# Keys and values of a banded attention, staged beside constants in idle memory and placed by DMA

## The chip, the cores and the metric

The kernel runs on one core of one Trainium2 chip. A core has a matrix engine (TensorE, PE in the profile), a vector engine (VectorE, DVE), an activation engine (ScalarE, ACT), GpSimd (POOL), a sequencer that only issues transfers here (SyncE, SP), 16 DMA engines, an on-chip memory of 128 partitions (SBUF) and eight accumulation banks of 128 x 512 float32 (PSUM) into which TensorE writes. The engines run their own instruction lists in order and wait for each other by semaphores. The metric is the device time of one execution in microseconds, lower is better.

## The reference

Four layers act on one residual stream x of 2048 tokens by 512 features in bfloat16: A, B, A, B, each with a layer norm in front. A is linear attention, B is softmax attention over a band of 256 tokens; both have 32 heads of 16 features.

```python
def _A_ref(x, wqkv, wo):                      # H = 32, Dh = 16
    q, k, v = split_heads(x @ wqkv)
    phi = lambda t: jnp.where(t > 0, t + 1, jnp.exp(t)) + 1e-6
    pq, pk = phi(q), phi(k)
    kv = jnp.einsum("bhsd,bhse->bhde", pk, v); z = jnp.einsum("bhsd->bhd", pk)
    num = jnp.einsum("bhqd,bhde->bhqe", pq, kv)
    den = jnp.einsum("bhqd,bhd->bhq", pq, z)[..., None] + 1e-6
    return merge_heads(num / den) @ wo
def _B_ref(x, wqkv, wo):                      # W = 256
    q, k, v = split_heads(x @ wqkv)
    scores = jnp.einsum("bhqd,bhkd->bhqk", q, k) * (Dh ** -0.5)
    p = _softmax(jnp.where(0 <= iq - ik < W, scores, -1e9))
    return merge_heads(jnp.einsum("bhqk,bhkd->bhqd", p, v)) @ wo
x = x + _A_ref(_layernorm(x), ...); x = x + _B_ref(_layernorm(x), ...)   # twice
```

(`split_heads` and `merge_heads` stand for the reshapes and transposes of the original.)

## The kernel before

**Tiling and stages.** The 2048 tokens are 16 tiles of 128, on the partitions where features are free and the other way round after a transpose. `build` (L325) writes five stages into one graph of operations: `layer_a_keys` (keys, values and queries of the first A layer), `barrier(1)`, `middle(2)`, `barrier(2)`, `middle(3)`. A barrier sums keys times values over all tiles (`a_kv`, L499), masks the sum, multiplies it with the output weights (M, L539) and forms the denominators. A `middle` finishes an A layer tile by tile (`a_out`, then `norm`, then the projections of layer B), runs layer B with the scores of a tile against this tile and the next two, and, in `middle(2)`, the key and value projections of the next A layer (`a_k`, `a_v`).

**Order.** Each operation has a key, in units of tiles (100 times the stage plus the tile plus an offset from PAR, L22), a cost, what it reads and writes, and the PSUM banks it needs. `schedule` (L87) plays the graph forward: each engine takes the ready operation with the smallest key, and operations named by `either` or `copy` go to ACT or DVE, whichever is free first. That gives one fixed order for each engine. `synchronise` (L219) turns it into semaphore waits: one counting semaphore for each compute engine, and one of 48 semaphores for each transfer. SP issues all transfers in order, so a transfer that waits holds those behind it.

**Keys of layer B.** The scores are matrix products with 32 rows in contraction, four side by side in the array. A group of 32 rows holds a pair of heads, so the keys of a pair must stand beside zeros: for each block of 64 tokens `kB` has 128 columns, 64 with only the first head's rows filled and 64 with only the second's. `b_qkv` (L584) projects the keys with the weights `wBp`, which GpSimd has permuted at the start (L403: in a group of 32, 16 rows of one head, then 16 of the other), and one DVE instruction (L595) reads the 128 x 512 result from PSUM twice over, times a per-partition 0 or 1 (`half`, L391 to L394), into the 1024 columns of `kB`. `kB` has four slots, tile t uses slot t % 4.

**Values of layer B.** The product of probabilities and values contracts over 128 rows: 64 tokens for the first head of a pair and the same 64 for the second. So `vB` has, for each block of 64 tokens and each pair, 34 columns: the first head's 16 values and a one in partitions 0 to 63, the second head's 16 values and a one in partitions 64 to 127, zeros elsewhere. GpSimd writes the zeros and ones once (L397 to L399). `b_v` (L597) makes the right layout in PSUM by 16 products with 64 columns each (L608), and two copies of 64 partitions (L614, shown as L444) bring it to `vB`, on ACT or DVE.

**Others that the change touches.** `norm` (L413) runs statistics (L416, L417), adds epsilon on DVE (`eps`, L418), takes the power -1/2 on GpSimd (L419), and normalizes on DVE (L420); a DMA transpose (L426) or TensorE turns the tile. `phi` (L474) is an ACT exponential (L478), a DVE minimum (L479) and a DVE combination (L480). The exponentials of layer B are L644, L645 and L678, its masks L651 and L685. `vA` (16 tiles by 512) holds the values of an A layer: written by `a_v` (L488), read by `a_kv` at the barrier, and idle in between.

Of the kernel before, what the change touches and what calls it, by code (L numbers as in the profile page):

```python
# [6 lines left out]
dt = mybir.dt  # L7
ACT = mybir.ActivationFunctionType
ALU = mybir.AluOpType
# [13 lines left out]
    lat_t=4300, cap_s=8, cap_d=2, cap_e=6, mode=100, sem=35, ring_x=3, wait_s=100, act_bias=-0.064, k_aq2=8.75, k_aq3=-3.0, k_akv=16.63, k_far2=1.412, k_far3=0.95, k_pv2=0.414, k_wo2=-0.276, k_next2=1.1, k_q2=3.26, k_ao2=4.701, k_kv2=2.436, k_v2=0.227, k_av2=17.25, k_ak2=0.108, pe_first2=1, pe_last2=1, k_pv3=0.864, k_wo3=1.497, k_next3=1.814, k_q3=3.411, k_ao3=3.603, k_kv3=2.867, k_v3=0.163, pe_first3=3, pe_last3=1,  # L23
# [23 lines left out]
class Graph:  # L47
    def __init__(self):
        self.ops, self.w, self.r = [], {}, {}
# [37 lines left out]
def schedule(g, par):  # L87
# [39 lines left out]
    while done < len(ops):  # L127
# [18 lines left out]
        for e in engines:  # L146
# [4 lines left out]
            held_back = False  # L151
            while ready[e]:
# [149 lines left out]
class Plan:  # L302
# [22 lines left out]
    def build(self):  # L325
        self.setup()
        self.layer_a_keys(1, 0)
        self.barrier(1)
        self.middle(2)
        self.barrier(2)  # L330
        self.middle(3)
# [6 lines left out]
    def setup(self):  # L338
# [52 lines left out]
        pool("c17", lambda e: e.iota(K.row[:], pattern=[[0, 1]], base=0, channel_multiplier=1), 163, 150, wr=[("row",)])  # L391
        self.on("DVE", "c18", lambda e: e.tensor_scalar(K.row2[:], K.row[:], 4, 1, op0=ALU.logical_shift_right, op1=ALU.bitwise_and), 14, (70, 150), rd=[("row",)], wr=[("row2",)])
        self.on("DVE", "c19", lambda e: e.tensor_copy(K.half[:, 1:2], K.row2[:]), 15, (70, 150), rd=[("row2",)], wr=[("half1",)])
        self.on("DVE", "c20", lambda e: e.tensor_scalar(K.half[:, 0:1], K.half[:, 1:2], -1.0, 1.0, op0=ALU.mult, op1=ALU.add), 16, (70, 150), rd=[("half1",)], wr=[("half",)])  # L394

        for s in range(4):
            pool("c21", lambda e, s=s: e.memset(K.vB[:, s, :, :, :], 0.0), 167, 1100, wr=[("vB", s)])  # L397
            pool("c22", lambda e, s=s: e.memset(K.vB[0:64, s, :, :, 16:17], 1.0), 168, 130, rd=[("vB", s)], wr=[("vB", s)])
            pool("c23", lambda e, s=s: e.memset(K.vB[64:128, s, :, :, 33:34], 1.0), 168, 130, rd=[("vB", s)], wr=[("vB", s)])  # L399
# [13 lines left out]
    def norm(self, t, key, xn_slot, out, wr, by_pe):  # L413
# [4 lines left out]
        self.on("DVE", "eps", lambda e: e.tensor_scalar(K.ve[:, t, :], K.mv[:, t, 1:2], LN_EPS, None, op0=ALU.add), key + 0.02, (66, 150), rd=[("mv", t)], wr=[("ve", t)])  # L418
# [165 lines left out]
    def b_qkv(self, t, s, key, key2):  # L584
# [10 lines left out]
        self.on("DVE", "bke", lambda e: e.tensor_tensor(K.kB[:, r, :, :, :], K.ps(pk).rearrange("p (b n) -> p b n", b=8).unsqueeze(2).to_broadcast([P, 8, 2, 64]), K.half[:].unsqueeze(1).unsqueeze(3).to_broadcast([P, 8, 2, 64]), ALU.mult), key + 0.05, dve(1024), rd=[("half",)], wr=[("kB", r)], ps=[pk])  # L595

    def b_v(self, t, s, key):  # L597
        K = self
        rd = [("xT", s)]
        r = t % 4  # L600
        pv = Tile(1, K.cls)

        def put(e):
            m = None
            for b in range(2):
                for c in range(4):
                    for a in range(2):
                        m = e.matmul(K.ps(pv)[64 * a:64 * a + 64, 256 * b:256 * b + 256], K.xT[:, s, c, 64 * b:64 * b + 64], K.wBv[:, c, 256 * a:256 * a + 256], start=c == 0, stop=c == 3, tile_position=(0, 64 * a))  # L608
            return m

        self.pe("bv", put, key, 8, 256, mode=(128, 64), rd=rd + [("wBv",)], ps=[pv])
        for a in range(2):
            rows = slice(64 * a, 64 * a + 64)
            self.copy("bve", pv, lambda a=a, rows=rows: K.vB[rows, r, :, :, 17 * a:17 * a + 16], lambda rows=rows: K.ps(pv)[rows, :].rearrange("p (b r d) -> p b r d", b=2, d=DH), key + 0.05, 512, wr=[("vB", r, a)], rd=[("vB", r)])  # L614

    def b_scores(self, j, f, key):
# [16 lines left out]
        self.pe("s", put, key, 1, sum(ns), mode=(32, 128), rd=[("kB", j % 4)] + [("XQ", t) for t in range(j, last + 1)], ps=ps)  # L633
# [21 lines left out]
    def b_far(self, j, key):  # L655
# [15 lines left out]
        self.pe("s", put, key, 1, 512, mode=(32, 128), occ=245, rd=[("kB", j % 4), ("XQ", j + 2)], ps=ps)  # L671
# [17 lines left out]
    def b_values(self, j, h, key):  # L689
# [5 lines left out]
        for f in (2 * h, 2 * h + 1):  # L695
# [10 lines left out]
            for i in range(max(0, j - 2), j + 1):  # L706
                rd += [("P", i % 3, f), ("vB", i % 4, 0), ("vB", i % 4, 1), ("vB", i % 4)]
                rd += [("P", i % 3, f, h_, b) for h_ in range(3) for b in (None, 0, 1)]
# [17 lines left out]

    def middle(self, ph):
        K = self
        K.cls = "D"
# [12 lines left out]

        for t in range(min(3, T)):
            front(t)
        self.b_v(0, 0, base - par["k_v"])
        for j in range(T):
# [16 lines left out]
            if last:  # L763
                self.on("SP", "out", lambda e, j=j: e.dma_start(K.out[0, j * P:(j + 1) * P, :], K.xres[:, j, :]), k + 0.1, (600, 2600), rd=[("xres", j)])
            else:
                k += par["k_next"] - par["k_wo"]
                self.norm(j, k, 3, lambda j=j: K.XQ[:, :, j * P:(j + 1) * P], [("XQ", j)], tail)
                self.a_k(j, k + par["k_ak"])
                self.a_v(j, base + par["k_av"] + 0.01 * j)


class Kernel(Plan):
# [16 lines left out]
    def run(self):  # L789
# [4 lines left out]
        with ExitStack() as cx:  # L794
# [7 lines left out]
            sb("stats", [T, 6], F32); sb("mv", [T, 2], F32); sb("ve", [T, 1], F32); sb("rs", [T, 1], F32)  # L802
            sb("ident", [P]); sb("ones", [P]); sb("bmask", [P]); sb("hot", [4, 32]); sb("spread", [4, 4, P]); sb("eps", [32])
            sb("tri", [2, 64]); sb("negh", [1], F32); sb("half", [2], F32); sb("row", [1], dt.int32); sb("row2", [1], dt.int32)
# [88 lines left out]
```

## Time and profile before

| | |
|---|---|
| runs (median of 3; lowest, highest) | 469.32 us; 468.39, 469.47 |
| the profiled execution: its own time; its span | 471.55 us; 469.8 us |
| mean granted TensorE clock | 0.969 |
| busy: PE, DVE, ACT, POOL | 409.5, 405.6, 370.4, 60.4 us |
| weight loads on PE | 284.0 us |
| DMA traffic | 19.11 MB, 41 GB/s in the mean |

Times in rows are microseconds from the start of the span. A group's row has the line, the engine, the operation, what it writes and reads, the shapes, how many (x), then the busy time and the mean of one in ns, then how long the engine stood idle just before such instructions and what released it. A timeline's row has the start, the length, and what ran. Busy times of stretches show which engine is full in which stage; a row of `PE` counts matmuls with their pipeline's end, `PEld` the weight loads.

### The profile page before, as it was taken

What the parts mean: (1) busy time and instruction counts of PE and PEld (TensorE: products, weight loads), DVE (VectorE), ACT (ScalarE), POOL (GpSimd) and SP (SyncE); (2) the same over time, 40 slices, a digit from 0 to 9 for tenths busy, and PEclk for the clock granted to TensorE, in tenths of its full rate; (3) what the DMA queues carried; (4) which work ended last, traced back from release to release, by engine and by line L of the source; (5) the groups of instructions that cost most, each with busy time, mean ns of one, the idle gap of its engine ahead of it and who ended that gap; (6) DMA issues with size and microseconds to landing.
All of it is one profiled execution on the core that took longest, in us unless ns stands there. A gap on an engine that the chain in (4) does not pass through costs nothing.

```text
span 469.8 us, 17818 instructions
## 1 busy us (share of the span) xinstructions
PE 409.5 (87%) x7937; PEld 284.0 (60%) x8004; DVE 405.6 (86%) x923; ACT 370.4 (79%) x550; POOL 60.4 (13%) x114
## 2 busy tenths in 40 slices
PE   3899989988888887999999998879899999998875
PEld 1455668656565555676666765756666657666543
DVE  4998699999999988998998749998999999998653
ACT  2365524989999979889999453599999999999982
POOL 8865000100101010000000000100000000000000
PEclk9899999999999999999999999998999999999776
DMA  8700002011131222122111100021222122121011
GB/s 274 265 0 1 1 1 37 13 32 29 35 37 36 36 36 36 36 37 35 25 26 27 28 9 1 4 22 35 48 25 59 39 35 48 36 47 36 25 33 39
DMA packets 47948, 19.11 MB, mean 41 GB/s; under 512 B 40192, under 2 KB 47360, under 8 KB 47872
## 3 DMA queue, kind: packets, MB, share of 16 engines
q1 hardware_dynamic: 47872, 17.97, 18.5%
q8 instruction: 63, 1.03, 0.9%
q14 instruction: 13, 0.11, 0.1%
HBM read 6.29 MB, written 2.10 MB: 18 GB/s over the span
## 4 chain that ended last, share of the span: by engine, by line
PE 38%; DVE 35%; ACT 20%; issue 2%; POOL 2%; DMA 1%; POOLq 0%
PE ps L455 13%; ACT pb L644 11%; PE ps L469 8%; PE ps L703 7%; DVE stats L416 4%; DVE xres L582 4%; PE ps L608 3%; ACT pb L678 3%; PE ps L630 3%; DVE pb L651 3%; DVE vB L444 3%; DVE kB L595 2%; DVE pqd L576 2%; DVE pb L685 2%; DVE tE L479 2%
## 5 line engine op out<-in xcount | busy, mean ns | idle before, releaser
L644 ACT ACTIVATE pb<-ps 128x1024 bf16<-128x1024 f32 x224 | 212.3, 1038 | 15.8 <-PE ps L630 15.0
L703 PEld LDWEIGHTS ps<-vB,pb 128*128 128x128 bf16 x2880 | 78.7, 96 | 21.7 <-DVE kB L595 3.3
L703 PE MATMUL ps<-vB,pb 128*128 128x34 bf16 x2880 | 84.9, 178 | 6.5 <-DVE o L715 1.4
L419 POOL TENSOR_TENSOR rs<-ve,negh 128x1 f32<-128x1 f32 x64 | 36.6, 571 | 356.2 <-DVE ve L418 354.8
L469 PE MATMUL ps<-xT,wBp 128*128 128x128 bf16 x1024 | 67.6, 220 | 3.5 <-ACT xT L439 1.4
L469 PEld LDWEIGHTS ps<-xT,wBp 128*128 128x128 bf16 x1024 | 58.8, 98 | 15.3 <-DVE xres L582 4.9
L455 PE MATMUL ps<-wA,XQ 128*128 128x512 bf16 x234 | 60.7, 392 | 5.8 <-DVE XQ L439 1.3
L478 ACT ACTIVATE tE<-ps 128x512 bf16<-128x512 f32 x64 | 39.0, 609 | 31.1 <-PE ps L455 14.6
L630 PE MATMUL ps<-XQ,kB 32*128 32x256 bf16 (+3 forms) x1024 | 50.6, 273 | 12.0 <-ACT pb L644 6.5
L651 DVE TENSOR_TENSOR pb<-pb,tri 128x512 bf16<-128x512 bf16 x128 | 53.1, 415 | 8.6 <-ACT pb L645 4.4
L678 ACT ACTIVATE pb<-ps 128x512 bf16<-128x512 f32 x112 | 58.7, 630 | 1.8 <-PE ps L668 1.6
L582 DVE TENSOR_TENSOR xres<-ps,xres 128x512 bf16<-128x512 f32 x64 | 43.7, 682 | 8.0 <-PE ps L455 7.0
L416 DVE BATCH_NORM_STATS2 stats<-xres 128x6 f32<-128x512 bf16 x64 | 43.4, 683 | 3.6 <-DMA xres<-in_A_x_dram 3.0
L595 DVE TENSOR_TENSOR kB<-ps,half 128x1024 bf16<-128x1024 f32 x32 | 38.8, 1211 | 1.3 <-PE ps L469 1.3
L455 PEld LDWEIGHTS ps<-wA,XQ 128*128 128x128 bf16 x256 | 21.9, 100 | 29.3 <-issue 4.1
L685 DVE TENSOR_TENSOR pb<-pb,tri 128x1024 bf16<-128x1024 bf16 x56 | 37.4, 679 | 2.4 <-ACT pb L678 2.4
L630 PEld LDWEIGHTS ps<-XQ,kB 32*128 32x128 bf16 x1024 | 15.3, 93 | 39.0 <-ACT pb L644 19.0
L455 PE MATMUL ps<-wBo,oT 128*128 128x512 bf16 x107 | 32.1, 411 | 7.2 <-DVE pqd L576 1.6
L608 PE MATMUL ps<-wBv,xT 128*64 128x256 bf16 x512 | 35.3, 283 | 1.7 <-DVE o L715 1.3
L479 DVE TENSOR_SCALAR tE<-tE 128x512 bf16<-128x512 bf16 x64 | 20.7, 325 | 17.4 <-ACT tE L478 17.1
L469 PE MATMUL ps<-XQ,wA 128*128 128x128 bf16 x512 | 34.9, 219 | 0.6 <-DVE recf L559 0.6
L444 DVE CAST vB<-ps 64x512 bf16<-64x512 f32 x44 | 30.4, 690 | 3.9 <-PE ps L608 2.5
(81 smaller groups left out, 489.0 us busy)
## 6 DMA issues: line engine op xcount, KB each, us to landing
out_dram<-xres SPq DMA_DIRECT2D x16, 128.0 KB, 1.7
wA<-in_A_wqkv_dram SPq DMA_DIRECT2D x3, 512.0 KB, 5.7
xres<-in_A_x_dram SPq DMA_DIRECT2D x2, 512.0 KB, 8.1
pb<-in_B_wqkv_dram SPq DMA_DIRECT2D x1, 1024.0 KB, 9.9
xres<-in_A_x_dram SPq DMA_DIRECT2D x3, 256.0 KB, 4.4
wAo<-in_A_wo_dram SPq DMA_DIRECT2D x1, 512.0 KB, 8.9
wBv<-in_B_wqkv_dram SPq DMA_DIRECT2D x1, 512.0 KB, 10.0
wBo<-in_B_wo_dram SPq DMA_DIRECT2D x1, 512.0 KB, 9.9
```

Source lines behind the costliest of these rows:

```text
L416: self.on("DVE", "stats", lambda e: e.bn_stats(K.stats[:, t, :], K.xres[:, t, :]), key, dve(512), rd=[("xres", t)], wr=[("stats", t)])
L455: m = e.matmul(K.ps(ps), lhs(c), rhs(c), start=c == 0, stop=c == 3)
L469: m = e.matmul(K.ps(ps)[:, f * P:(f + 1) * P], w(c, f), xT(c), start=c == 0, stop=c == 3)
L582: self.on("DVE", "res", lambda e: e.tensor_tensor(K.xres[:, t, :], K.ps(po), K.xres[:, t, :], ALU.add), key, dve(512), rd=[("xres", t)], w ...
L595: self.on("DVE", "bke", lambda e: e.tensor_tensor(K.kB[:, r, :, :, :], K.ps(pk).rearrange("p (b n) -> p b n", b=8).unsqueeze(2).to_broadca ...
L608: m = e.matmul(K.ps(pv)[64 * a:64 * a + 64, 256 * b:256 * b + 256], K.xT[:, s, c, 64 * b:64 * b + 64], K.wBv[:, c, 256 * a:256 * a + 256], ...
L630: m = e.matmul(K.ps(ps[gq])[:, 256 * b:256 * b + ns[b]], K.kB[rows, j % 4, 2 * f + b, :, :], K.XQ[rows, f, q:q + ns[b]], start=True, stop= ...
L644: return e.activation(x, bank().rearrange("p g (b n) -> p g b n", b=2), ACT.Exp, bias=0.0, scale=0.25)
L651: return e.tensor_tensor(x, x, K.tri[:, 0, :].unsqueeze(1).unsqueeze(1).to_broadcast([P, 4, 2, 64]), ALU.mult)
L678: return e.activation(K.pb[:, sl, 2 * h:2 * h + 2, :, o:o + 64], i, ACT.Exp, bias=0.0, scale=0.25)
L685: return e.tensor_tensor(x, x, K.tri[:, 1, :].unsqueeze(1).to_broadcast([P, 16, 64]), ALU.mult)
L703: m = e.matmul(K.ps(ps)[:, 34 * u:34 * u + 34], K.pb[:, (b // 2) % 3, gq, f, o:o + P], K.vB[:, (b // 2) % 4, b % 2, r, :], start=i == 0, s ...
```

## The change

1. **Keys.** The weights are permuted so that the rows of a pair's two heads alternate (even rows the first head, odd rows the second). One copy (ACT or DVE, `either`) brings the 128 x 512 result into a staging area, in blocks of 64 with 64 constant zeros between them. Two transfers on SP, one for the even partitions and one for the odd, read 1024 columns, the odd ones 64 columns further left, so that zeros fall where the other head's columns are, and write `kB`. 64 rows of 2048 bytes each.
2. **Values.** Plain token-major product (`tok`: four matmuls of 512 columns) in place of 16; one copy of 128 partitions into a second staging area, with 34 columns for each head: 16 values, a constant one, and zeros. Four transfers (block of tokens by head) read 544 columns and write a quarter of `vB`. 64 rows of 1088 bytes each.
3. **Staging area.** It is `vA`, idle in the `middle` stages: tiles 0 to 5 for keys and 6 to 11 for values, two halves each, used in turn. GpSimd writes its zeros and ones at the start of both `middle` stages. `a_v` now stands behind the loop of `middle(2)` in the graph, so that it waits for the last transfer that reads the tiles that it writes.
4. `half`, `row` and the constants of `vB` go away.
5. `eps` goes from DVE to POOL.
6. **Order.** New offsets in PAR for all stages; a second kind of offset (`o_...`) shifts the key of an operation by its name and stage; `wait_s`, which `schedule` uses to hold TensorE back for scores, goes from 100 to 200. (`same` is 0 and does nothing.)

```diff
-    lat_t=4300, ..., wait_s=100, act_bias=-0.064, k_aq2=8.75, k_aq3=-3.0, k_akv=16.63, ...
+    same=0.0, lat_t=4300, ..., wait_s=200, act_bias=-0.378, k_aq2=7.28, k_aq3=-8.85, k_akv=28.47,
+    k_far2=2.522, k_far3=1.248, k_pv2=0.64, ..., k_q2=2.944, k_ao2=4.686, k_kv2=2.41, k_v2=0.148, k_av2=18.49,
+    ..., k_q3=5.029, k_ao3=3.649, k_kv3=2.494, k_v3=-0.211, ..., o_bke3=-0.456, o_ve2=-1.945, o_kd2=-0.187, o_kd3=0.99,
...
-        o = Op(len(self.ops), engs, emit, key, name)
+        o = Op(len(self.ops), engs, emit, key + self.shift.get(name, 0.0), name)
...
-        for s in range(4):
-            pool("c21", lambda e, s=s: e.memset(K.vB[:, s, :, :, :], 0.0), 167, 1100, wr=[("vB", s)])
...
-                    K.wBp[:, q, k, :].rearrange("p (r a d) -> p r a d", a=2, d=DH),
+                    K.wBp[:, q, k, :].rearrange("p (r d a) -> p r a d", a=2, d=DH),
...
-        self.on("DVE", "eps", lambda e: e.tensor_scalar(K.ve[:, t, :], K.mv[:, t, 1:2], LN_EPS, ...), key + 0.02, (66, 150), ...)
+        self.on("POOL", "eps", lambda e: e.tensor_scalar(K.ve[:, t, :], K.mv[:, t, 1:2], LN_EPS, ...), key + 0.02, (190, 260), ...)
...
-        self.on("DVE", "bke", lambda e: e.tensor_tensor(K.kB[:, r, :, :, :], K.ps(pk)...to_broadcast([P, 8, 2, 64]), K.half[:]..., ALU.mult), key + 0.05, dve(1024), ...)
+        flat = lambda: K.vA[:].rearrange("p t d -> p (t d)")[:, 1536 * st:1536 * st + 1152]
+        self.either("bke", lambda e, eng: e.activation(flat()[:, 64:1088].rearrange("p (b a n) -> p b a n", b=8, a=2)[:, :, 0, :], K.ps(pk)..., ACT.Copy) if eng == "ACT" else
+                    e.tensor_copy(flat()[:, 64:1088]...[:, :, 0, :], K.ps(pk)...), key + 0.05, 512, wr=room, ps=[pk])
+        for a in range(2):
+            def put(e, a=a):
+                src, dst = flat(), K.kB[:]
+                ss, ds = src.ap[0][0], dst.ap[0][0]
+                i = bass.AP(src.tensor, src.offset + a * ss + 64 * (1 - a), [[2 * ss, 64], [1, 1024]])
+                o = bass.AP(dst.tensor, dst.offset + a * ds + 1024 * r, [[2 * ds, 64], [1, 1024]])
+                return e.dma_start(o, i)
+            self.on("SP", "kd", put, key + 0.06, (540, K.par["lat_t"]), rd=room, wr=[("kB", r, a)])
...
-        self.pe("bv", put, key, 8, 256, mode=(128, 64), rd=rd + [("wBv",)], ps=[pv])
-        for a in range(2):
-            self.copy("bve", pv, lambda a=a, rows=rows: K.vB[rows, r, :, :, 17 * a:17 * a + 16], ...)
+        pv = self.tok("bv", t, lambda c: K.xT[:, s, c, :], lambda c: K.wBv[:, c, :], [("xT", s), ("wBv",)], key)
+        self.copy("bve", pv, lambda: flat()[:, 17:1105].rearrange("p (h d) -> p h d", d=34)[:, :, 0:16], ..., key + 0.05, 512, wr=room)
+        for b in range(2):
+            for a in range(2):
+                self.on("SP", "vd", lambda e, a=a, b=b: e.dma_start(
+                    K.vB[64 * a:64 * a + 64, r, b, :, :].rearrange("p r d -> p (r d)"),
+                    flat()[64 * b:64 * b + 64, 17 + 527 * a:17 + 527 * a + 544]), key + 0.06, (550, K.par["lat_t"]), rd=room, wr=[("vB", r, a, b)])
...
+        for i in range(2):
+            self.on("POOL", "zero", lambda e, i=i: e.memset(flat(1536 * i, 1152), 0.0), base - 5, (600, 660), wr=self.room[i])
+        for i in range(2):
+            self.on("POOL", "zero", lambda e, i=i: e.memset(flat(3072 + 1536 * i, 1105), 0.0), base - 5, (600, 660), wr=self.roomv[i])
+            self.on("POOL", "zero", lambda e, i=i: e.memset(flat(3072 + 1536 * i + 17, 1088)...[:, :, 16:17], 1.0), base - 5, (150, 200), ...)
...
                 self.a_k(j, k + par["k_ak"])
+        if not last:
+            for j in range(T):
                 self.a_v(j, base + par["k_av"] + 0.01 * j)
```

More of the change, by code (lines that the diff above doesn't have):

```diff
@@ L151, in schedule @@
             held_back = False
+            if e == "PE" and par["same"]:
+                ready[e] = [(ops[i].key + (par["same"] if ops[i].mode != last_mode[0] else 0.0), i) for _, i in ready[e]]
+                heapq.heapify(ready[e])
             while ready[e]:
@@ L611, in b_v @@
-        self.pe("bv", put, key, 8, 256, mode=(128, 64), rd=rd + [("wBv",)], ps=[pv])
-        for a in range(2):
-            rows = slice(64 * a, 64 * a + 64)
-            self.copy("bve", pv, lambda a=a, rows=rows: K.vB[rows, r, :, :, 17 * a:17 * a + 16], lambda rows=rows: K.ps(pv)[rows, :].rearrange("p (b r d) -> p b r d", b=2, d=DH), key + 0.05, 512, wr=[("vB", r, a)], rd=[("vB", r)])
+        st = t % 2
+        room = self.roomv[st]
+        flat = lambda: K.vA[:].rearrange("p t d -> p (t d)")[:, 3072 + 1536 * st:3072 + 1536 * st + 1105]
@@ L631, in put @@
             return m
-        self.pe("s", put, key, 1, sum(ns), mode=(32, 128), rd=[("kB", j % 4)] + [("XQ", t) for t in range(j, last + 1)], ps=ps)
+        self.pe("s", put, key, 1, sum(ns), mode=(32, 128), rd=[("kB", j % 4, 0), ("kB", j % 4, 1)] + [("XQ", t) for t in range(j, last + 1)], ps=ps)
         sl = j % 3
@@ L706, in b_values @@
             for i in range(max(0, j - 2), j + 1):
[L707 removed]
+                rd += [("P", i % 3, f)] + [("vB", i % 4, a, b) for a in range(2) for b in range(2)]
                 rd += [("P", i % 3, f, h_, b) for h_ in range(3) for b in (None, 0, 1)]
@@ L725, in b_out, with phase @@
         self.resid(j, po, key + 0.05)
+    def phase(self, ph):
+        self.g.shift = {k[2:-1]: v for k, v in self.par.items() if k[:2] == "o_" and k[-1] == str(ph)}
     def middle(self, ph):
         K = self
+        self.phase(ph)
         K.cls = "D"
```

49 lines of the change are left out of this document (28 added, 21 removed).

## The prediction

> **What bounds the kernel now.** The page's first table has PE and DVE about equally busy and ACT less, an average over stages with different limits. So I read the busy times of stretches next, cut where the work changes (first column the stretch, second its length; the columns after that as in the first line).
>
> ```profile
> core 0: us, PE busy (x) PEld busy (x) DVE busy (x) ACT busy (x) POOL busy (x), PEclk, DMA share, GB/s
> 0.00:60.00 60.00, 48.08 (x450) 28.23 (x456) 45.88 (x124) 28.97 (x49) 33.04 (x66) 0.97 0.33 106
> 60.00:90.00 30.00, 27.09 (x428) 21.32 (x432) 29.25 (x66) 16.01 (x24) 3.44 (x6) 1.00 0.13 20
> 90.00:250.00 160.00, 140.61 (x3051) 97.87 (x3078) 149.39 (x344) 148.33 (x206) 13.46 (x23) 1.00 0.21 34
> 250.00:282.00 32.00, 31.32 (x495) 22.36 (x500) 19.98 (x50) 19.73 (x46) 1.64 (x3) 1.00 0.07 15
> 282.00:302.00 20.00, 17.11 (x267) 13.04 (x270) 19.85 (x44) 8.36 (x16) 2.19 (x4) 1.00 0.01 2
> 302.00:320.00 18.00, 14.83 (x273) 10.08 (x272) 16.59 (x36) 15.34 (x20) 1.09 (x2) 0.94 0.19 24
> 320.00:430.00 110.00, 102.41 (x2375) 73.45 (x2382) 102.62 (x219) 105.58 (x136) 5.49 (x10) 1.00 0.22 42
> ```
>
> DVE alone is full in 60 to 90 (29.25 of 30) and 282 to 302. In 90 to 250, the steady part of the first middle, DVE and ACT are both at 93%. PE alone is full in 250 to 282, where it makes up the waiting value and query projections. In 320 to 430, the steady part of the second middle, ACT, DVE and PE stand at 96, 93 and 93%.
>
> Which part of ACT can't move is in the groups of its instructions, of 90 to 250 (first row) and 320 to 430 (the others). A tile has four L678 (L673 to L680), so 14 and 11 tiles pass, at 11.4 and 10.0 us each.
>
> ```profile
> L678 ACT ACTIVATE pb<-ps 128x512 bf16<-128x512 f32 x56 | 29.7, 641 | 0.7 <-PE ps L668 0.7
> ...
> L644 ACT ACTIVATE pb<-ps 128x1024 bf16<-128x1024 f32 x87 | 82.1, 1026 | 4.4 <-PE ps L630 4.0
> L678 ACT ACTIVATE pb<-ps 128x512 bf16<-128x512 f32 x44 | 22.7, 618 | 0.1
> ```
>
> The exponentials of the second middle take (82.1 + 22.7) / 11 = 9.53 us of each 10.0: a floor that the change doesn't touch. It can win at most 0.47 us a tile there; the first middle has more room.
>
> **The change part by part.** *What goes and what comes on DVE and ACT.* Rows of the groups, whole run:
>
> ```profile
> L595 DVE TENSOR_TENSOR kB<-ps,half 128x1024 bf16<-128x1024 f32 x32 | 38.8, 1211 | 1.3 <-PE ps L469 1.3
> L444 DVE CAST vB<-ps 64x512 bf16<-64x512 f32 x44 | 30.4, 690 | 3.9 <-PE ps L608 2.5
> L444 ACT ACTIVATE vB<-ps 64x512 bf16<-64x512 f32 x20 | 12.1, 606 | 2.5 <-PE ps L608 1.7
> L444 DVE CAST XQ<-ps 128x512 bf16<-128x512 f32 x18 | 12.3, 683 | 0.4 <-PE ps L469 0.3
> ```
>
> Out of each of the 32 tiles goes one key instruction, 1.21 us, on DVE only, and two value copies, (30.4 + 12.1) / 32 = 1.33 us. In come two copies of 512 columns, of the form of the XQ row: 0.68 on DVE, and on ACT 0.61 as the vB copies there, say 0.65. That saves 1.21 + 1.33 - 1.30 = 1.24 us a tile.
>
> Epsilon leaves DVE. Its row says 144 ns, but the next instruction starts 0.06 us after it:
>
> ```profile
> 66.48 0.14 DVE L418 TENSOR_SCALAR ve<-mv 128x1 f32<-128x1 f32 x1
> 66.54 0.68 DVE L416 BATCH_NORM_STATS2 stats<-xres 128x6 f32<-128x512 bf16 x1
> ```
>
> I count 0.06: two a tile in the first middle, one in the second. A tile is 1.36 and 1.30 us lighter. The POOL epsilon isn't in the trace; POOL's pow on the same shape takes 0.55 (row below), so the chain from statistics to xn grows by at most that, and may shrink by the place in DVE's list that it no longer waits for. It runs over a tile ahead; I take 0.
>
> *TensorE.* Sixteen value matmuls go, four of 512 columns come:
>
> ```profile
> 401.24 1.06 PE L608 MATMUL ps<-wBv,xT 128*64 128x256 bf16 x16
> ...
> 63.76 1.03 PE L455 MATMUL ps<-M,pqd 128*128 128x512 bf16 x4
> ```
>
> 1.06 against 1.03 us: nothing. But PE gets waits. A wait on a transfer costs its queue an instruction of its own:
>
> ```profile
> L822 PEldq EVENT_SEMAPHORE x72: 51/51/51, 7.9 to 426.9; - x72
> ```
>
> Six more transfers a tile make up to 6 x 51 ns = 0.31 us a tile, nothing where the queue has run ahead.
>
> *The new transfers.* SBUF to SBUF is not in the trace. Nearest are the 128 KB stores and the 128 x 512 transposes, first how long SP is held (ns, lowest, median, highest), then the landing:
>
> ```profile
> L764 SPq DMA_DIRECT2D out_dram<-xres x16: 332/332/365, 326.7 to 467.6; - x16
> ...
> DMA to landing us min/median/max: 1.7/1.7/2.4
> ...
> L426 SPq DMA_TRANSPOSE oT<-o x30: 1189/1195/1913, 93.1 to 458.7; - x30
> ...
> oT<-o SPq DMA_TRANSPOSE x30, 2.5
> ```
>
> I take the store's price, being nearest in kind: SP held 6 x 0.33 = 2.0 us a tile, with three transposes 2.0 + 3.6 = 5.6 of 11.4. The other end, the transpose's 1.19 for each, is a rival below. A keys' chain gets issue plus landing, 0.33 x 2 + 1.7 = 2.4 us (3.2 with 2.5). Does anything wait for that? At the start of the first middle:
>
> ```profile
> 72.13 1.22 DVE L595 TENSOR_TENSOR kB<-ps,half 128x1024 bf16<-128x1024 f32 x1
> ...
> 80.44 0.40 PE L630 MATMUL ps<-XQ,kB 32*128 32x256 bf16 x8
> ```
>
> 7.1 us lie between the end of the first key instruction and the first scores, which wait for queries of later tiles; later the lead is 2.4 tiles by PAR. Values have over a tile. So this latency costs 0. If the lead were gone it would be 2.4 to 3.2 us, once.
>
> *What queues behind the new waits.* A key transfer waits for its copy, a value transfer for its copy and for the last reader of the `vB` slot. Behind it on SP wait transposes (xT for the projections, oT for the output) and stores; behind a late transpose waits PE, in order, and behind PE ACT. What slack has a transpose?
>
> ```profile
> 402.34 1.20 SPq L426 DMA_TRANSPOSE xT<-xn  x1
> ...
> 407.18 1.06 PE L469 MATMUL ps<-xT,wBp 128*128 128x128 bf16 x16
> ```
>
> Issued at 402.34 and landed 2.5 later, it feeds a projection at 407.18 at the earliest: 2.3 us. I cost the queueing at 0, with a rival.
>
> *Staging.* The zeros and ones are six memsets a middle, four of about 1.03 us as in the first row and two short ones, about 4.6 us of POOL:
>
> ```profile
> L397 POOL MEMSET vB<- 128x1088 bf16 x4 | 4.1, 1029 | 0.2
> ...
> 281.12 0.39 PE L506 MATMUL ps<-pk,vA 128*128 128x128 bf16 x4
> ...
> 291.67 0.55 POOL L419 TENSOR_TENSOR rs<-ve,negh 128x1 f32<-128x1 f32 x1 [21.33 <-DVE ve L418]
> ```
>
> They wait for the last product that reads `vA` (281.5) and fit before POOL's next work (291.67). But a DVE instruction can be held beside a memset:
>
> ```profile
> 41.44 0.95 POOL L408 MEMSET pb<- 128x1024 bf16 x1
> 41.55 0.98 DVE L479 TENSOR_SCALAR tE<-tE 128x512 bf16<-128x512 bf16 x1
> ...
> L479 DVE TENSOR_SCALAR tE<-tE x64: 226/290/985, 12.4 to 302.2; 128x512 bf16<-128x512 bf16 x64
> ...
> L651 DVE TENSOR_TENSOR pb<-pb,tri x128: 360/415/448, 82.9 to 460.3; 128x512 bf16<-128x512 bf16 x128
> ```
>
> L479 takes 0.29 in the median and 0.98 here. One or two may be caught at each barrier, 0 to 1.4 us.
>
> *`a_v` behind the room.* The 16 value projections of the next A layer fill PE gaps late in the first middle. Now twelve must wait for transfers of tiles 14 and 15. They were late already: copies into `vA` in a stretch near the end (columns PE, PEld, DVE, ACT), and the last key instruction:
>
> ```profile
> 250.00:260.00 10.00, 0.00 (x0) 0.00 (x0) 0.67 (x1) 1.79 (x3) 1.00 0.09 19
> ...
> 226.87 1.22 DVE L595 TENSOR_TENSOR kB<-ps,half 128x1024 bf16<-128x1024 f32 x1
> ```
>
> The last key instruction begins at 226.87, which frees the six key tiles by 231; four copies come only in 250 to 260, so the limit hardly binds: 0. At worst those four slip into the stretch where PE is full, at 1.03 us each: +4.
>
> *The new order.* Its offsets change every engine's list, and no row prices that. What it could win alone is idle time of the fullest engines, ACT's 11.7 us in 90 to 250 and 4.4 in 320 to 430; what it could lose is bounded by no row, so I allow the same. I take 0.
>
> *The sum, by stretch.*
> - 0 to 60: 16 epsilons off a busy DVE, 16 x 0.06: -1 (0 to -2.5).
> - 60 to 90, DVE full, ACT half idle: keys begin here (72.13), about four in 18 us; each 0.57 lighter on DVE, or 1.21 if the copy goes to ACT: 2.3 to 4.8, less up to 1.4 for the memsets: -2 (+1 to -4.8).
> - 90 to 250: 14 x 1.36 = 19 us off two engines at 93%; shared evenly 9.5. PE at 88% gets up to 14 x 0.31 = 4.3, so I take -8 (-4 to -10).
> - 250 to 282, PE full: 0 (0 to +4).
> - 282 to 302: 0 (-0.3 to +1.4).
> - 302 to 320: 1.8 tiles x 1.30 / 2: -1 (0 to -2.3).
> - 320 to 430: DVE gets 11 x 1.30 lighter, but ACT keeps 9.53 of 10.0 a tile. The chain of work that ended last shows what DVE's part is worth:
>
> ```profile
> 350.48 1.01 PE ps L608 x16
> 351.52 0.68 DVE vB L444
> ...
> 352.89 0.70 DVE vB L444
> ```
>
> In every second tile both value copies are on it, 0.69 a tile; one copy that nothing waits for takes their place, less 0.31 of waits: 0.38 x 11 = -4 (0 to -5.2, ACT's floor).
> - 430 to the end: the last tiles' values, 0.68 a tile lighter: -0.5 (0 to -1).
>
> Sum -16.5: 471.55, the profiled execution's own time, becomes 455. It lies 2.2 above the median of the runs shown, so for the median 469.32 - 16.5, 453.
>
> **The rivals.** *TensorE becomes the bound.* For: 102.41 of 110 busy, and more waits. Then 320 to 430 wins nothing, 90 to 250 half of its term: -16.5 + 4 + 4 gives 461. Against: PE's busy time counts each group's pipeline end; its weight loads are busy for 73.45 of 110. The Trainium skill, "Trainium Kernel Development and Optimization", section Performance Expectations, calls matmul busy time a bad measure of closeness to the limit and the busy share of weight loads a good one; by that PE keeps a third free and this rival falls away.
>
> *GpSimd holds DVE off.* L479 beside the memset is the case for it. 64 epsilons at half a pow, 0.27, are 17 us, the memsets 9.2, and 4.1 (L397) go: 22 us of POOL more. L651 and L479, 128 x 0.415 + 64 x 0.29 = 72 of the 384 us in the DVE column above, would meet it a fifth of the time: +4, so 457. The Trainium skill, "SBUF — State Buffer", section Who interferes with whom, says that GpSimd and DVE lock each other out of a shared port for a whole instruction, DVE's instructions with two SBUF inputs included where GpSimd reads. The trace agrees for L479, but of 128 L651 with two inputs none is longer than 448 ns, though a pow takes 550.
>
> *Everything falls into place.* The first middle shrinks by 10, the second to ACT's floor, the start by 4.8 and 2.5: 447, and to 443 with idle time that the new order closes.
>
> *Slower: SP's list holds up the transposes.* Place: both steady stretches. If an SBUF copy held SP as long as a transpose, nine at 1.19 are 10.7 us a tile, more than the 10.0 to aim at; or a transfer waits for a copy that comes late. Price: what a transpose loses beyond its 2.3 us of slack is lost on PE and ACT, in about 25 tiles. The gain of 16.5 is eaten at 0.66 us a tile, so from a delay of 3.0 us; at 3.5 it is 453 + 25 x 1.2 = 483. Against: 0.33 us for the store.
>
> **How the numbers follow.** Forecast 453: 0.55 (own range 448 to 458). TensorE's bound, 461: 0.16. GpSimd's hold, 457: 0.08. All in place, 443 to 447: 0.11. Slower, 483: 0.07. That nothing happens, since a new wait takes what DVE gives, 468 to 470: 0.03. About 0.3%, 1.4 us, can be told from no change. Faster: 0.55 + 0.16 + 0.08 + 0.11 = 0.90, of which I give 0.02 to each other side for the new order: 0.86; same 0.05; slower 0.09. The range, 442 to 466, leaves out the last two cases and holds the bounds of the terms but for several worst ends at once.
>
> **What would show it.** ACT in the steady stretch of the second middle at 97% or more; 128x512 key copies of 0.6 to 0.7 us; DVE under 90% there; 264 waits on PE's queue in place of 72; transposes landing in 2.5 us as now; key and value transfers off the chain of work; 250 to 282 no longer than now. I am wrong if PE waits on `kB` or `vB` transfers or on transposes, if SP is held over 1 us by a direct transfer, or if the end of the first middle grows by several us.

## The result, and the profile after

| | before | after |
|---|---|---|
| runs: median of 4 (lowest, highest) | 468.86 us (467.3, 469.47) | 453.74 us (453.23, 454.15) |
| the profiled execution: its time; its span | 471.55; 469.8 us | 453.23; 451.5 us |
| mean granted clock | 0.969 | 0.983 |

The ratio is 0.9682, with a 95% interval of 0.9654 to 0.971: 15 us less in the medians, 18.3 between the two spans. Some 3 of the 18.3 us aren't the change's: the profiled execution of before had a mean granted clock of 0.969 and lies 2.7 us above its median; two other executions of the same kernel at 0.967 took 473 us, those at 0.985 468 to 470. The forecast was 453. Busy times and the chain, from the page of after:

```profile
span 451.5 us, 17346 instructions
...
PE 400.2 (89%) x7540; PEld 267.7 (59%) x7620; DVE 372.4 (82%) x835; ACT 364.6 (81%) x539; POOL 83.2 (18%) x177
...
ACT 38%; PE 31%; DVE 23%; POOL 4%; issue 3%; POOLq 0%; DVEq 0%
```

The busy times fell by 9 us on PE, by 33 on DVE and by 6 on ACT, and POOL's rose by 23. What that is worth is read by stretch (after, columns as in the prediction's table, cut where the work of after changes):

```profile
core 0: us, PE busy (x) PEld busy (x) DVE busy (x) ACT busy (x) POOL busy (x), PEclk, DMA share, GB/s
0.00:60.00 60.00, 48.53 (x450) 27.84 (x456) 46.47 (x104) 30.18 (x52) 36.43 (x75) 1.00 0.33 106
60.00:90.00 30.00, 27.67 (x413) 20.81 (x419) 27.10 (x60) 18.39 (x29) 4.94 (x12) 1.00 0.32 69
90.00:235.00 145.00, 130.36 (x2743) 86.83 (x2769) 128.88 (x299) 136.67 (x185) 19.95 (x46) 1.00 0.42 84
235.00:270.00 35.00, 34.00 (x556) 23.07 (x562) 23.22 (x54) 21.53 (x51) 7.12 (x12) 1.00 0.12 25
308.00:414.00 106.00, 100.11 (x2234) 67.72 (x2256) 94.64 (x206) 105.35 (x133) 9.97 (x20) 1.00 0.43 99
```

In 60 to 90 DVE is no longer full; in 90 to 235, the steady part of the first middle, ACT is at 94%, PE at 90 and DVE at 89; in 235 to 270 PE is full as before. In 308 to 414, the steady part of the second middle, ACT is busy 105.35 of 106 us. The chain of work of a part of it:

```profile
by line: ACT pb L659 76.1%; ACT pb L693 23.5%; PE ps L645 1.4%; issue 0.2%
...
324.06 1.96 ACT pb L693 x4
326.02 0.01 issue
326.04 7.60 ACT pb L659 x8
333.63 1.96 ACT pb L693 x4
335.60 0.01 issue
335.61 7.60 ACT pb L659 x8
343.21 1.96 ACT pb L693 x4
```

Eight exponentials of 128x1024 (7.60 us), then four of 128x512 (1.96), and again from the start, with 0.01 us between them: a tile takes 9.57 us (324.06 to 333.63). Nothing else is on the chain there, so this stretch is an ACT list without gaps.

Where the 18.3 us of the two spans come from, by events that both traces have: the masking of the sum at each barrier (on DVE, L535 before) and the first and last score product of each middle (PE, L630 before):

| part | before | after | change | forecast |
|---|---|---|---|---|
| start to the first mask | 54.9 | 54.3 | -0.6 | -1 |
| to the first scores | 25.5 | 24.8 | -0.7 | -2 |
| first middle, first to last scores | 179.7 | 169.4 | -10.3 | -8 |
| to the second mask | 21.6 | 21.1 | -0.5 | 0 |
| to the first scores of the second middle | 22.2 | 22.4 | +0.2 | 0 |
| second middle, first to last scores | 154.8 | 149.9 | -4.9 | -1, -4 |
| to the end | 11.0 | 9.6 | -1.4 | -0.5 |

Now the new operations. Groups of after:

```profile
L605 DVE CAST vA<-ps 128x512 bf16<-128x512 f32 x24 | 16.5, 687 | 0.8 <-PE ps L475 0.8
...
L604 ACT ACTIVATE vA<-ps 128x512 bf16<-128x512 f32 x8 | 5.0, 621 | 2.4 <-PE ps L475 2.3
...
L767 POOL MEMSET vA<- 128x1152 bf16 x4 | 4.2, 1057 | 6.8 <-PE ps L515 6.7
```

Of the key copies, 24 are on DVE and 8 on ACT, at 0.687 and 0.621 us (forecast 0.68 and 0.61). Single lines of after, as they answer for a line of the kernel (ns, lowest, median, highest; first and last start): waits on transfers, the transfers of keys and values, the transposes, the stores, and instructions that POOL might hold or be held by.

```profile
L852 PEldq EVENT_SEMAPHORE  x137: 51/51/571, 8.4 to 440.1; - x137
L852 DVEq EVENT_SEMAPHORE  x58: 21/50/50, 91.8 to 420.0; - x58
...
L613 SPq DMA_DIRECT2D kB<-vA x64: 464/596/1992, 72.2 to 412.3; - x64
...
DMA to landing us min/median/max: 1.9/2.1/3.8
...
L627 SPq DMA_DIRECT2D vB<-vA x128: 461/596/2042, 83.3 to 432.0; - x128
...
L432 SPq DMA_TRANSPOSE oT<-o x30: 1189/1274/2461, 95.4 to 441.2; - x30
...
L792 SPq DMA_DIRECT2D out_dram<-xres x16: 332/584/589, 316.2 to 449.2; - x16
...
L424 POOL TENSOR_SCALAR ve<-mv x64: 208/222/526, 6.1 to 400.8; 128x1 f32<-128x1 f32 x64
...
L485 DVE TENSOR_SCALAR tE<-tE x64: 228/286/1147, 13.5 to 302.7; 128x512 bf16<-128x512 bf16 x64
...
L666 DVE TENSOR_TENSOR pb<-pb,tri x128: 360/420/452, 81.9 to 443.1; 128x512 bf16<-128x512 bf16 x128
```

SP is held 0.596 us by a direct transfer in the median, not 0.33, and longer by the old store too (0.584, before 0.332).

### The profile page after: what moved, and what is told of

Read it like the earlier page. It is cut to its first block, busy times and chain, and to the rows that moved or that the text cites. A ratio compares the mean times of both kernels' runs of the same rounds, so it can differ in the third digit from the quotient of the medians.

```text
span 451.5 us, 17346 instructions
## 1 busy us (share of the span) xinstructions
PE 400.2 (89%) x7540; PEld 267.7 (59%) x7620; DVE 372.4 (82%) x835; ACT 364.6 (81%) x539; POOL 83.2 (18%) x177
## 4 chain that ended last, share of the span: by engine, by line
ACT 38%; PE 31%; DVE 23%; POOL 4%; issue 3%; POOLq 0%; DVEq 0%
ACT pb L659 28%; PE ps L461 14%; PE ps L475 7%; ACT pb L693 6%; PE ps L718 4%; DVE stats L422 3%; PE ps L645 3%; DVE xres L588 3%; DVE xn L426 2%; DVE pk L486 2%; DVE XQ L486 2%; DVE tE L485 2%; POOL rs L425 2%; ACT pb L660 2%; DVE pb L700 2%
## 5 line engine op out<-in xcount | busy, mean ns | idle before, releaser
L718 PEld LDWEIGHTS ps<-vB,pb 128*128 128x128 bf16 x2880 | 80.1, 96 | 18.4 <-DVE vA L450 2.7
L424 POOL TENSOR_SCALAR ve<-mv 128x1 f32<-128x1 f32 x64 | 17.3, 270 | 299.1 <-DVE mv L423 297.6
L666 DVE TENSOR_TENSOR pb<-pb,tri 128x512 bf16<-128x512 bf16 x128 | 53.7, 419 | 18.4 <-ACT pb L659 12.3
L425 POOL TENSOR_TENSOR rs<-ve,negh 128x1 f32<-128x1 f32 x64 | 38.0, 594 | 5.3
L461 PE MATMUL ps<-wBo,oT 128*128 128x512 bf16 x106 | 30.8, 406 | 5.2 <-DVE xn L426 1.4
L426 DVE TENSOR_SCALAR xn<-xres,mv,rs 128x512 bf16<-128x512 bf16 x64 | 28.6, 453 | 6.3 <-POOL rs L425 5.8
L475 PEld LDWEIGHTS ps<-XQ,wA 128*128 128x128 bf16 x512 | 30.2, 98 | 4.7 <-DVE XQ L486 0.6
L461 PE MATMUL ps<-wBv,xT 128*128 128x512 bf16 x110 | 29.6, 380 | 3.3 <-DVE o L730 1.0
```

Source lines behind the costliest of these rows:

```text
L425: self.on("POOL", "pow", lambda e: e.tensor_tensor(K.rs[:, t, :], K.ve[:, t, :], K.negh[:], ALU.pow), key + 0.03, (540, 590), rd=[("ve", t ...
L461: m = e.matmul(K.ps(ps), lhs(c), rhs(c), start=c == 0, stop=c == 3)
L475: m = e.matmul(K.ps(ps)[:, f * P:(f + 1) * P], w(c, f), xT(c), start=c == 0, stop=c == 3)
L666: return e.tensor_tensor(x, x, K.tri[:, 0, :].unsqueeze(1).unsqueeze(1).to_broadcast([P, 4, 2, 64]), ALU.mult)
L718: m = e.matmul(K.ps(ps)[:, 34 * u:34 * u + 34], K.pb[:, (b // 2) % 3, gq, f, o:o + P], K.vB[:, (b // 2) % 4, b % 2, r, :], start=i == 0, s ...
```

## The experiments

The change holds three things that could bring the time: less work on DVE and ACT (keys; values), and a new order. Two theories stood against each other. *Weight*: the time comes from the lighter parts, and the order is worth nothing by itself, as the prediction took it. *Order*: the new offsets bring it, and would do so with the old parts.

**First series: one part of the change at a time, with fixed offsets.** e1 is the kernel before with the changed offsets. e2 is the changed kernel with the offsets of before. e3 and e4 keep the changed offsets and put the old values, or the old keys, back.

```diff
 # e1, on the kernel before                    # e2, on the changed kernel
-    lat_t=4300, ..., act_bias=-0.064, ...
+    same=0.0, lat_t=4300, ..., act_bias=-0.378, ...
+    self.g.shift = {...}
 # e3, on the changed kernel
-    pv = self.tok("bv", ...); self.copy("bve", pv, ...) once; four transfers "vd"
+    self.pe("bv", put, ...)  16 matmuls; two self.copy("bve", ...) of 64 partitions into vB
 # e4, on the changed kernel
-    self.either("bke", ...); two transfers "kd"
+    self.on("DVE", "bke", ... tensor_tensor(K.kB[...], ..., K.half[...]), dve(1024), ...)
```

(e2 is the same edit of PAR the other way round.)

> The kernel before with all offsets of the changed one (the new PAR, the shifts by name, wait_s 200) and nothing else: old keys, old values, epsilon on DVE. Theory 'weight' (the gain is the work that left DVE and ACT; the order by itself is worth nothing): within 4 us of before, 465 to 473. Rival 'order' (the new order closes idle time and brings most of the gain): 458 or less.

> The changed kernel with the old offsets, no shifts by name, wait_s 100: only keys, values, staging and epsilon are new. Theory 'weight': at least 9 of the 15 us, 453 to 460. Rival 'order': 463 or more.

> The changed kernel with the old values (16 matmuls of 64 columns, two copies of 64 partitions, constants of vB written once); keys, epsilon and offsets as changed. Theory 'weight': what is left saves 0.57 of the 1.25 us a tile on DVE and ACT besides epsilon, so about half the gain, 459 to 464, and ACT in the steady part of the second middle stays short of its floor (9.6 us a tile or more). Rival 'one part carries it': 454 to 456 here and 467 or more with the values alone, or the other way round.

> The changed kernel with the old keys (one DVE instruction of 1024 columns, times a 0 or 1 by partition; old permutation of the weights); values, epsilon and offsets as changed. Theory 'weight': what is left saves 0.68 of the 1.25 us a tile, somewhat over half the gain, 458 to 463. Rival 'one part carries it': as at the keys alone, the other way round.

| | time | ratio to before (95%) |
|---|---|---|
| e1, order alone | 483.17 | 1.0259 (1.0178 to 1.034) |
| e2, parts alone | 468.48 | 0.998 (0.9949 to 1.0011) |
| e3, keys alone, changed order | 478.95 | 1.0176 (1.0105 to 1.0246) |
| e4, values alone, changed order | 474.72 | 1.0103 (1.0031 to 1.0175) |

Neither theory holds. The new order makes the old parts 14 us slower (483.17 against 468.93), and the new parts in the old order win nothing that can be told from 0. By its stages, e2 wins 3.1 us in the first middle (176.6 against 179.7) and loses 2.2 in the second (157.0 against 154.8). `schedule` makes new lists for each of these kernels, but by offsets that were found for other parts, and the loss is in its plan already: run by itself, it ends the kernel before at 454.4 us of its own time, e1 at 466.2, e2 at 453.5 and the changed kernel at 438.6. So a part that is put in or taken out under fixed offsets shows the misfit beside the part's worth. That holds for e3 and e4 as much: they say little of keys and values.

**Second series: each set of parts with an order of its own.** The revised theory: the lighter parts permit a shorter time, and an order that fits them is needed to reach it. So offsets were found anew for each set, in the same way: from the offsets of before, some 3,000 random changes, each kept where the kernel's own planner (`schedule`) then ended earlier; for f1, g1 and g2 the better of two such searches. Only PAR differs (and, in f1, the second kind of offset comes in as in e1).

```diff
-    same=0.0, lat_t=4300, ..., wait_s=200, act_bias=-0.378, k_aq2=7.28, ...
+    same=0.0, lat_t=4300, ..., act_bias=..., k_aq2=..., ...     # f1 old parts, f2 e3's, f3 e4's, f4 all new
```

> The kernel before (old keys, old values, epsilon on DVE) with offsets found for it: some 3,000 random changes from the old offsets, shifts by name allowed, each kept where the kernel's own planner ended earlier. The next three kernels have theirs found in the same way from the same start. Theory 'weight sets the reach, an order that fits is needed to get there': 460 to 466, so that 6 us or more of the changed kernel's gain are out of reach for the old parts. Rival 'order' (any parts get there with an order of their own): within 3 us of f4.

> New keys and epsilon, old values, offsets of its own (as f1). Theory 'weight': between f1 and f4, 456 to 462. Rival 'order': within 3 us of f1 and f4.

> New values and epsilon, old keys, offsets of its own (as f1). Theory 'weight': between f1 and f4, at or below f2, since 0.68 us a tile go against 0.57: 454 to 460. Rival 'order': within 3 us of f1 and f4.

> The changed kernel's parts with offsets of their own, found as f1's from the old offsets. Theory 'weight': 451 to 458, near the changed kernel's 453.7 although the offsets are others; the steady part of the second middle at 9.6 us a tile. Rival 'these offsets' (the changed kernel's own set is what counts): 460 or more.

**Third series: what of the values it is.** The new values bring another product (4 matmuls for 16) and one copy for two. g1 and g2 separate the two, each again with offsets of its own, and with the old keys as in f3.

```diff
 # g1, on f3: the 16 old matmuls, one copy of 128 partitions, two transfers
-    pv = self.tok("bv", ...)
+    self.pe("bv", put, key, 8, 256, mode=(128, 64), ...)
     self.copy("bve", pv, ... 512 columns of 128 partitions ...)
-    for b in range(2):
-        for a in range(2): self.on("SP", "vd", ... 544 columns ...)
+    for a in range(2):     self.on("SP", "vd", ... 1088 columns ...)
 # g2, on f3: the 4 new matmuls, two copies
-    self.copy("bve", pv, lambda: flat()[:, 17:1105]..., ...)
+    for b in range(2):
+        rows = slice(64 * b, 64 * b + 64)
+        self.copy("bve", pv, lambda rows=rows: flat()[rows, 17:1105]..., lambda rows=rows: K.ps(pv)[rows, :]..., ...)
```

> As f3 (old keys, epsilon on POOL), but the values come from the old 16 matmuls of 64 columns; one copy of 128 partitions into a staging area, and two transfers of 64 rows of 2176 bytes into vB. Offsets of its own, found as f1's. Which half of the values' change counts? Theory 'copies' (DVE and ACT are rid of 0.68 us a tile): like f3, 453 to 458. Rival 'matmuls' (16 narrow matmuls in another mode cost TensorE more than their busy time says): like f1, 461 to 466.

> As f3, but with the copy cut into two of 64 partitions, so that DVE and ACT have as many value copies as before; the four plain matmuls and the four transfers stay. Offsets of its own, found as f1's. Theory 'copies': like f1, 460 to 466. Rival 'matmuls': like f3, 453 to 458.

The stage lengths are taken between the same events as above. All but before and f1 have epsilon on POOL and `a_v` behind the loop:

| | keys; matmuls; value copies | time | ratio to before (95%) | start to first mask | first middle | second middle |
|---|---|---|---|---|---|---|
| before | old; old; 2 | 468.86 | | 54.9 | 179.7 | 154.8 |
| f1 | old; old; 2 | 464.71 | 0.989 (0.9847 to 0.9933) | 53.0 | 176.1 | 154.3 |
| f2 | new; old; 2 | 464.47 | 0.99 (0.9871 to 0.993) | 58.0 | 175.8 | 152.0 |
| g2 | old; new; 2 | 463.36 | 0.9869 (0.9819 to 0.9919) | 53.3 | 172.6 | 157.7 |
| f3 | old; new; 1 | 454.15 | 0.9679 (0.9644 to 0.9715) | 53.8 | 172.3 | 146.9 |
| g1 | old; old; 1 | 453.86 | 0.9668 (0.9628 to 0.9709) | 53.2 | 171.0 | 149.6 |
| f4 | new; new; 1 | 454.2 | 0.9688 (0.9656 to 0.9719) | 54.8 | 169.7 | 148.8 |
| after | new; new; 1 | 453.74 | 0.9682 (0.9654 to 0.971) | 54.3 | 169.4 | 149.9 |

f1, f3, f4, g1 and g2 fell in the ranges expected by their theories; f2 missed its 456 to 462. f4 is as fast as the changed kernel with other offsets, so it is not that one set that counts.

Three kernels with two value copies lie at 463.4 to 464.7, four with one at 453.7 to 454.2. g2 stages its values in `vA` and sends them by the same four transfers as f3, so it isn't the staging that brings this. Over the two middles, one copy for two brings 9 to 11 us in each pairing: f1 to f3 -3.8 and -7.4, g2 to f3 -0.3 and -10.8, g2 to g1 -1.6 and -8.1, f2 to f4 -6.1 and -3.2. (The profiled execution of g2, 465.35, lies 2 us above its median, so its stages are read a little long.) The matmuls bring nothing (f3 to g1, -0.3). The keys bring 0.7 to 2.6 us over the middles (f1 to f2 -0.3 and -2.3; f3 to f4 -2.6 and +1.9), which is little beside what an order or one execution differs from the next: f2 loses 5 us to f1 before the first mask, where values and keys of layer B do not run. The order alone, on the old parts, brings 4 us (f1). With f3, most of the gain is had without the new keys.

In g2 the trace shows what a second copy does. Groups of g2 in 315 to 405, nine tiles of the second middle: the copies and the key and query projections.

```profile
L479 PE MATMUL ps<-xT,wBp 128*128 128x128 bf16 x288 | 19.2, 220 | 2.5 <-ACT vA L454 1.2 <-DVE xres L592 0.3
L479 PEld LDWEIGHTS ps<-xT,wBp 128*128 128x128 bf16 x288 | 16.1, 98 | 8.8 <-DVE vA L454 3.7 <-DVE xres L592 2.5 <-ACT vA L454 2.0
L454 DVE CAST vA<-ps 64x512 bf16<-64x512 f32 x10 | 6.9, 693 | 2.4 <-ACT vA L454 1.7 <-PE ps L465 0.5
L454 ACT ACTIVATE vA<-ps 64x512 bf16<-64x512 f32 x8 | 5.3, 657 | 0.0
```

One such tile in the timeline of g2:

```profile
349.02 0.70 ACT L454 ACTIVATE vA<-ps 64x512 bf16<-64x512 f32 x1
...
349.75 0.70 DVE L454 CAST vA<-ps 64x512 bf16<-64x512 f32 x1 [0.26 <-ACT vA L454]
...
350.51 0.90 PEld L479 LDWEIGHTS ps<-xT,wBp 128*128 128x128 bf16 x16 [0.63 <-DVE vA L454]
```

The copies sit on two engines and still run one after the other: `Graph.add` makes each operation on a bank wait for the one before it on that bank. So the bank is held longer, and the next projection, which needs one, waits for it: 3.7 + 2.0 = 5.7 us in nine tiles on PE, by its weight loads. From its first weight load to the end of its last copy the product takes 2.49 us in the median, in f3 1.77 (worked out from the starts and ends in the traces after the second barrier). But ACT carries eight of the eighteen copies, 5.3 us or 0.59 a tile. With the floor of 9.53 that makes 10.12, and a tile takes 10.15 (between the first L686 of one tile and of the next, 367.92 and 378.07), in f3 9.60; ACT is busy 89.03 of the 90 us. So g2's second middle is an ACT list again, with a copy in it, and PE's 5.7 us may cost nothing. That accounts for 0.55 us a tile, some 6 of the 10.8 us; the rest is open. Both kinds of copy are on the chain of these 90 us:

```profile
by line: ACT pb L652 46.8%; ACT pb L686 16.6%; PE ps L479 8.3%; DVE vA L454 5.4%; ACT vA L454 4.9%; PE ps L711 4.0%; DVE xres L592 3.9%; DVE pb L693 3.8%; PE ps L638 2.7%; issue 1.5%; DVE recf L569 1.0%; PE ps L465 0.9%; DVE pb L659 0.8%; D
```

The same groups of g1, with one copy, on DVE in all nine tiles:

```profile
L479 PEld LDWEIGHTS ps<-xT,wBp 128*128 128x128 bf16 x288 | 16.8, 98 | 5.8 <-issue 2.1 <-DVE xres L592 2.0 <-DVE pb L666 1.6
L454 DVE CAST vA<-ps 128x512 bf16<-128x512 f32 x9 | 6.2, 689 | 0.1
```

Nobody waits for these copies, and ACT carries none. In f1 the price is paid elsewhere. Its chain in the same 90 us:

```profile
by line: PE ps L467 20.4%; PE ps L715 14.8%; PE ps L481 13.7%; ACT pb L656 11.7%; PE ps L642 9.7%; DVE vB L456 7.6%; PE ps L620 6.7%; DVE o L727 4.3%; DVE pb L663 2.9%; DVE rc L726 2.7%; DVE xn L432 2.1%; issue 1.6%; DVE kB L607 1.3%; ACT X
```

There the copies on DVE (L456, 7.6%) take turns on the chain with PE, and nothing is full all the time (PE 84.9, DVE 85.1 and ACT 86.0 of 90 us). That a second copy costs about 10 us is shown by the times. That it does so by ACT's time is shown for the steady tiles of g2; that the bank's longer hold costs anything besides is not shown. Why 0.57 us less on a key is worth so much less than 0.68 on the values is not shown. One reason fits the profiles: after the values' change the second middle is at ACT's floor (f3 busy 89.06 of the 90 us), so keys could only win in the first.

**Is the floor what is left?** g3 adds to the changed kernel, once for each tile of the second middle, a DVE instruction of 0.68 us whose result nobody reads; at the floor it should cost nothing. g4 is the changed kernel with its offsets searched on from where they are.

```diff
 # g3, on the changed kernel, in the loop over tiles of middle(3)
+            if ph == 3:
+                self.on("DVE", "load", lambda e, j=j: e.bn_stats(K.dum[:, j % 2, :], K.wBv[:, 0, :]), base + j + 0.5, dve(512), ...)
 # g4: PAR alone
```

> The changed kernel with one more DVE instruction a tile in the second middle (statistics of 512 columns of a constant, 0.68 us, result unused); offsets as changed. Theory 'floor' (the second middle waits only for ACT's exponentials): at most 2 us slower than the changed kernel, 453 to 456. Rival 'DVE's weight still counts there': 16 x 0.68 = 11 us, 460 or more.

> The changed kernel with offsets searched on from its own, in the way of f1. Theory 'floor': the second middle can't win, the first a little: 451 to 455. Rival 'order': 448 or less.

g3 took 455.37, 0.97 (0.9656 to 0.9745), and tells nothing of the floor. Its row:

```profile
L787 DVE BATCH_NORM_STATS2 dum<-wBv x16: 671/679/686, 37.8 to 55.8; 128x6 f32<-128x512 bf16 x16
```

All 16 ran between 37.8 and 55.8 us: they wait for nothing but a weight, and the planner gave them to DVE wherever it was free in the first stage, which became 2.1 us longer (56.4 to the first mask, after 54.3). The second middle, which carries none of it and has the same lists as in the changed kernel, is longer too (151.5, after 149.9): by so much, 1.6 us, the length of a stage differs between two executions, and the stage lengths above are each of one. A load on a stage must depend on the work of that stage. g4 took 454.86, 0.9693 (0.9641 to 0.9745): another order, no gain. None of these kernels is faster than the changed one by more than the runs can tell.

## Why the prediction was right, and which of its steps were not

The median lies 0.7 us above the forecast, and the second middle came out for the reason given: ACT's floor, forecast 9.53 us a tile, measured 9.57. That the whole sum fits is in part luck, by the first two points. Point by point:

- **The new order, "I take 0": the step that failed.** It isn't a term that is added to the weight. Without it the lighter parts gave nothing that can be told from 0 (e2, 0.998); with an order of their own they gave about 15 us (f4, after). And on the old parts an order found anew brings 4 us by itself (f1). The sum gave all of the 16.5 us to the weight and came out right because the change came with an order that fits. The row that should have raised doubt was there: ACT and DVE were both at 93% in the first middle, neither full, so the rest of their time was waits, and taking weight off doesn't remove a wait by itself.
- **The weight, 1.36 and 1.30 us a tile, all of one worth: wrong in its parts.** The second value copy's share carries nearly all of it; keys and epsilon bring 0.7 to 2.6 us over the middles, and in the medians 0.2 and less (f1 to f2, where 5 us are lost before the first mask, and f3 to f4, where epsilon is on POOL in both).
- **90 to 250, -8; 320 to 430, -4: about right.** -10.3 and -4.9 for the whole middles. In the second, a steady tile took 10.12 us (9.74 and 10.50 in turn, between the first L678 of one tile and of the next) and takes 9.57: 0.55 won, where the prediction took 0.38 and, counting 11 whole tiles in 110 us, allowed 0.47. The start, 60 to 90, was taken too high (-2; -0.7).
- **Value matmuls 0: right**, by f3 against g1.
- **264 waits on PE's queue: 137.** The price of one, 51 ns, held. The 192 new transfers brought only 65 more waits there, and 58 (before 2) on DVE, of 50 ns, that weren't forecast.
- **SP held 0.33 us for each transfer: 0.596, mis-sized**, and landing 2.1 for 1.7; the transposes land in 2.5 in the median, as before. Six transfers are 3.6 us a tile, not 2.0. In the 100 us that begin 40 us after the second mask, the lengths of all issues on SP add up to 75 us (before 28). In this order that cost nothing: no transfer is on the chain behind the first mask.
- **The transposes' slack of 2.3 us: wrong.** It is one tile's: in before, the transpose issued at 382.11 lands 4.4 us later, 0.4 before its projection at 386.95. And it is the slack in one order, not of the kernel. In f4, with SP held 82.5 of those 100 us, a transpose comes far later than the 3.0 us from which the slower rival was to eat the gain (`xn`, the issues on SP, the projection):

```profile
342.16 0.41 DVE L425 TENSOR_SCALAR xn<-xres,mv,rs 128x512 bf16<-128x512 bf16 x1
343.00 1.27 SPq L431 DMA_TRANSPOSE oT<-o  x1
344.31 1.53 SPq L791 DMA_DIRECT2D out_dram<-xres  x1
345.89 1.12 SPq L612 DMA_DIRECT2D kB<-vA  x2
347.05 1.27 SPq L431 DMA_TRANSPOSE xT<-xn  x1
...
352.69 1.96 PE L474 MATMUL ps<-xT,wBp 128*128 128x128 bf16 x32
```

  `xn` ends at 342.57 and its transpose is issued at 347.05, 4.5 us later (over the second middle 4.8 in the median, 11.4 at most), landing takes 2.5 more, and the projection comes at 352.69, still 3 us after that. f4 is no slower for it. **The slower rival** so fell in the steady part of orders that fit (f4 has one transpose on its chain, at 298.68, ahead of it). In e2, with the same transfers in the old order, its mechanism does show. There a transpose issued at 313.53, 3.3 us after its `xn` and behind four value transfers, is on the chain of work, and so is a later one; together they are 7.4 us of it. The later one, as the chain has it:

```profile
379.83 3.77 DMA xT<-xn
```

  That is far from 483, but the second middle of e2 is 2.2 us longer than that of before; how much of this is the transposes' is not shown.
- **TensorE as the bound: fell.** PE is busy 100.11 of 106 us in the steady second middle and ACT reaches its floor all the same; weight loads are busy 67.72. The Trainium skill, "Trainium Kernel Development and Optimization", section Performance Expectations, has the latter as the better measure; the trace of after agrees. PE isn't far behind, though: in f4, which is as fast, PE's work makes up 79.5% of the chain in 315 to 405, with its weight loads busy 58.89 of these 90 us and ACT 88.49.
- **GpSimd's hold: small, as forecast.** L485 is stretched to 1147 ns at most, but all 64 together take 20.8 us (before 20.7); the two-input L666 never goes beyond 452 ns.
- **`a_v` behind the room and the zeros at the barriers: 0, right.** The parts around the second mask change by -0.5 and +0.2.
- **What would show it:** ACT over 97% and DVE under 90% in the steady second middle came (99.4 and 89.3%), and keys and values are off its chain; SP stayed under 1 us for a direct transfer in the median, single ones took up to 2.04.

Open: why the keys' share is worth so little; by which way a second copy costs its time in f1 and f2, and whether the bank's longer hold has a part in it; and how much of the last 3 us between these kernels is a matter of the search. A load that is tied to the second middle's own work would test the floor, and wasn't tried.

## What to carry over

In a kernel whose instruction lists are planned ahead, a part is worth something only with an order planned for it: undo a part and plan again, or the run measures the misfit. A copy of 64 partitions took as long here as one of 128 (0.69 us on DVE), so two halves cost twice and, where a planner chains all users of a bank, hold it longer; one copy in place of two carried most of what the parts brought. Slack read from one order is that order's own, and isn't a bound on a delay in another.

## What was not expected of the hardware

- What holds SP is not the kind of a transfer alone. The store of 128 KB, unchanged, held it 0.332 us in the median before, 0.584 in after with six more transfers a tile, and 0.347 in g1 with two more; but e2, with the same six as after, has 0.349, so it isn't the number of transfers alone. Why is open.
- An SBUF to SBUF transfer of 64 rows landed 2.1 us after its issue in the median, whether of 68 or of 128 KB (L627 and L613); g1's, of 136 KB, took 2.5. The 128 KB store to memory took 1.7 before and 2.0 in after.
- GpSimd's own small instructions vary too: epsilon, 222 ns in the median, takes up to 526.
